# Linear attention into two MLPs on one core: the second batch's norms as rows through DRAM

## The chip, the cores and the metric

The kernel runs on one core of a Trainium2 chip, as one program. The metric is the device time of that program in microseconds (us). Before the change it is 1420.68 us, the median of three runs that lie between 1420.35 and 1421.77.

## What is computed

```
kv  = einsum('bhsd,bhse->bhde', k, v)            # 8 batches, 8 heads, 576 positions, 64 wide
out = einsum('bhsd,bhde->bhse', q, kv)
rms = sqrt(mean(out * out, axis=-1) + 1e-6)
x   = (out / rms * g_norm)                       # as 4608 tokens x 512
h   = x @ w_in;  x = (h * cos(h)) @ w_out        # 512 -> 2048 -> 512
a = x @ w1;  b = x @ w2                          # 512 -> 1024
result = ((a * b) @ w3) @ w_out2                 # 1024 -> 1024 -> 512
```

Everything is float32 outside. A product that has to be exact to float32 is made of three matrix products, with each operand cut into a high part (a copy in the fp32r type) and a low part (the operand less its high part).

## The kernel before, in words

A *unit* is half a batch: 288 tokens, units 0 and 1 are batch 0, units 2 and 3 batch 1. A *pair* p (0 to 3) is two heads, which fill the 128 partitions. A *block* is 512 tokens of the first MLP: block 0 is all of unit 0 and 224 tokens of unit 1, block 1 is 64 tokens of unit 1, unit 2, and 160 tokens of unit 3.

A *step* is one block of 512 tokens against 128 columns of w_in: `emit_h` issues its twelve matmuls (four slices c of the 512 inputs, three products each) on PE, ACT then rounds h/2pi to r (L619), DVE forms u from h and r (L620), ACT takes the sine of u (L636), and DVE multiplies it with h (L642). The first eight steps (h_0 to h_7) belong to block 0, the ninth (h_8) is the first of block 1. It reads the tile x_1, which needs the normalised output of the second batch. x is made from o (the attention's output) by a multiplication with the reciprocal norms, a copy to the high part on ACT (L910) and a subtraction for the low part (L911).

Weights come as *chunks*: a chunk is loaded as 64-bit words (`Chunk.load`), turned to floats in five operations (`Chunk.convert`: one on ACT at L156, four on DVE at L157, L158, L161 and L166), and then put: the high part on ACT (L122), the low part (L124) on DVE for the first four chunks and on GpSimd for the rest. Chunk i0 is w_in0 for step 0, and so on.

Batch 0 is done first (`first_batch`, L489). For each pair: k·v products on PE (`emit_kv`), their copy to a block diagonal on ACT (`copy_kv`), the output for both units (`emit_whole`, tile "out"), squares on ACT (`emit_square`), the sums of squares on PE into a narrow tile (`emit_sums`, tile "ms_first": 96 tokens down, 48 columns), and o kept on ACT (`emit_keep`). Then `norms` runs eleven small operations on DVE, and `emit_rows` spreads the norms over 64 partitions each by 12 small PE products for each unit and pair (tile "spread"), from which DVE scales o.

Batch 1 is woven into the first eight steps (`first_steps`, L565): its outputs, squares and sums lie one pair to a step in steps 0 to 3; `norms` follows in step 4, and the spreading and the scaling of o by DVE in steps 4 to 6, before h_8.

All engines execute in the order in which the code is written (the schedule is manual). SP's queue issues most DMAs in order, and each issue waits until the DMA eight places ahead of it has landed. So an instruction that waits holds up all that stand behind it on its engine.

Of the kernel before, what the change touches and what calls it, by code (L numbers as in the profile page):

```python
# [33 lines left out]
def kernel(  # L34
# [218 lines left out]
    rest_home = ap.tile([P, NPAIR // 2, 2, 2, P], F32, name="kvrest")  # L253

    def load_rest(b):
        t = kv_rest.setdefault(b, rest_home)
        for h in range(2):
            queue(NHALF * b).dma_start(
                out=t[0:TAIL, :, h], in_=kv_tail[b, TAIL * h:TAIL * (h + 1)]
            )  # L260
# [131 lines left out]
    def load_first():  # L392
# [15 lines left out]

        qs(0, 0, nc.scalar)
        qs(0, 1, nc.scalar)  # L410
# [4 lines left out]
        kv(0, 0, nc.sync)  # L415
        load_rest(0)
        kv(0, 1, nc.sync)
        prefetch(1)
        kv(0, 2, nc.sync)
        prefetch(2)  # L420
        qs(0, 2, nc.sync)
        prefetch(3)
        kv(0, 3, nc.sync)
        prefetch(4)
        qs(0, 3, nc.sync)
        for p in range(NPAIR):
            if p == 2:
                load_rest(1)
            kv(1, p, nc.sync)
        for p in range(NPAIR):  # L430
            qs(1, p, nc.sync)
            if p == 1:
                prefetch(8)
# [16 lines left out]
    def column(u, k, p):  # L450
        return ((u % NHALF * NT3 + k) * NPAIR + p) * 2
# [23 lines left out]
    def emit_rows(u, p, ps, y, spread, scaled=True):  # L475
        for k in range(NT3):
            at = column(u, k, p)
            for h in range(2):
                mm = nc.tensor.matmul(
# [4 lines left out]
        if scaled:  # L484
            o = o_sb[u][:, p, :]
            nc.vector.tensor_tensor(o, o, ps[:, 0:HALF], ALU.mult)
        return mm.ins

    def first_batch(spread, x, y, t):  # L489

        sums = ps_h.tile([P, 512], F32, tag="h", name="ms_first")
        units = range(NHALF)
        count = [1, 1, 1, 1]

        def pieces(n):
            made = [c.convert() for c in chunks[state["conv"]:state["conv"] + n]]
            state["conv"] += n
            for st in made:
                next(st)
            return made  # L500

        def rest_of(made):
            for _ in range(4):
                for st in made:
                    next(st)

        emit_kv(0, 0)
        copy_kv(0)
        made = None
        for p in range(NPAIR):  # L510
# [6 lines left out]
            if p == 0:  # L517
                made = pieces(count[0])
            if p < 3:
                rest_of(made)  # L520
            if p > 0:
                put(1)
# [9 lines left out]
            if p == 2:  # L532
                rest_of(pieces(count[3]))
            if p < 2:
                made = pieces(count[p + 1])
        for p in range(NPAIR):
            emit_kv(1, p)
            if p < 2:
                copy_kv(p)
        norms(sums, x, y, t)  # L540
        put(1)
        for p in (2, 3):
            copy_kv(p)
        for p in range(NPAIR + 1):
            if p < NPAIR:
                for u in units:
                    ps = ps_acc.tile(
                        [P, 512], F32, tag=f"acc{(2 * p + u) % 4}", name=f"spread_{u}_{p}"
                    )
                    emit_rows(u, p, ps, y, spread)  # L550
            if p == 0:
                for v in range(NHALF, 2 * NHALF):
                    out_bank(v, 0)
            if p > 0:
                split_x(0, p - 1)
# [9 lines left out]
    def first_steps(spread, x, y, t):  # L565

        units = range(NHALF, 2 * NHALF)
        spread_ps = {}
# [18 lines left out]
        def rows(p):  # L587
            for v in units:
                spread_ps[v, p] = two_banks(v, p, f"spread_{v}_{p}")
                emit_rows(v, p, spread_ps[v, p], y, spread, False)  # L590
# [1355 lines left out]
```

## Time and profile before

| | |
|---|---|
| median of 3 runs | 1420.68 us |
| the profiled execution's own time | 1422.03 us |
| its span | 1419.8 us |
| PE busy | 1401.1 us (99%) |
| DVE, ACT, POOL busy | 1004.3, 716.7, 568.6 us |
| chain of waits, by engine | PE 83%, DMA 5%, DVE 5%, POOL 2% |

The span is what lies between the first and the last instruction; the execution's own time holds 2.2 us more. PE is TensorE, DVE VectorE, ACT ScalarE, POOL GpSimd, SP the queue that issues DMAs; a q behind a name means that engine's issuing side. By the profile's windows, PE is busy 25.2 of the first 34.3 us, 34.2 of the next 34.4, and 1271.1 of the 1279.8 us from 140 us on. The chain of waits is the list of what each thing waited for last, followed back from the end. Where it names PE without a break, PE had work all the time, and every microsecond of PE work taken out or put in there moves the end.

### The profile page before, as it was taken

To read this page: it belongs to the slowest core of one execution; us is meant where nothing else is said; L and a number is where in the kernel's file an instruction comes from. 1 tells how busy PE (TensorE), PEld (TensorE's weight loads), DVE (VectorE), ACT (ScalarE), POOL (GpSimd) and SP (SyncE) were. 2 spreads that over 40 slices of the span, in tenths; PEclk is the share of its full clock that TensorE was granted. 3 is DMA by queue.
4 is the path that set the end of the run, shared out by engine and by line. 5 is a ranking of instruction groups with operands and counts; after the bars stand their busy time and mean duration, and the time that the engine had idled before them with its cause. 6 is when DMAs were issued, how large, how long until landed. Compare 5 with 4: busy or idle time off the path is not lost.

```text
span 1419.8 us, 23399 instructions
## 1 busy us (share of the span) xinstructions
PE 1401.1 (99%) x8376; PEld 1233.3 (87%) x8376; DVE 1004.3 (71%) x1555; ACT 716.7 (50%) x1338; POOL 568.6 (40%) x444
## 2 busy tenths in 40 slices
PE   7999999999999999999999999999999999999998
PEld 6877777777787888988888888999999999999998
DVE  5786575675778856888988957687775757855553
ACT  5665565545656655455555535443442334555553
POOL 1173763685385522132222428885760433100000
PEclk9999999999999999999999999999999999999999
DMA  9365987987798998999999982554445344775662
GB/s 338 130 232 171 338 258 220 300 281 247 240 320 305 324 345 294 319 348 326 371 334 358 363 298 103 159 158 139 140 134 149 97 144 144 248 273 216 252 219 101
DMA packets 210548, 345.55 MB, mean 243 GB/s; under 512 B 19104, under 2 KB 120576, under 8 KB 210048
## 3 DMA queue, kind: packets, MB, share of 16 engines
q1 hardware_dynamic: 209728, 343.48, 71.2%
q8 instruction: 65, 1.06, 0.3%
q10 hardware_dynamic: 704, 0.59, 0.1%
q14 instruction: 51, 0.42, 0.1%
HBM read 205.89 MB, written 138.11 MB: 242 GB/s over the span
## 4 chain that ended last, share of the span: by engine, by line
PE 83%; DMA 5%; DVE 5%; POOL 2%; issue 2%; ACT 1%; SPq 1%; ACTq 0%; DVEq 0%; POOLq 0%
PE X L1090 13%; PE X L1420 13%; PE h L916 8%; PE oX L1522 7%; PE h L917 7%; PE h L918 7%; PE V L1420 7%; PE V L1090 6%; PE oV L1522 4%; PE Y L1420 3%; PE Y L1090 3%; PE oY L1522 2%; PE event L297 1%; DMA g<-ta 1%; DVE g_hl L124 1%
## 5 line engine op out<-in xcount | busy, mean ns | idle before, releaser
L916 PE MATMUL h<-x,w_in 128*128 128x512 f32 x576 | 229.7, 399 | 1.3 <-DVE u L1740 0.9
L917 PE MATMUL h<-x,w_in 128*128 128x512 f32 x576 | 224.7, 390 | 0.7 <-DVE x L911 0.7
L918 PE MATMUL h<-x,w_in 128*128 128x512 f32 x576 | 224.6, 390 | 0.0
L1420 PE MATMUL X<-xc,w 128*128 128x384 f32 x1152 | 215.9, 334 | 0.7 <-ACT s L1428 0.6
L1420 PEld LDWEIGHTS X<-xc,w 128*128 128x128 f32 x1152 | 201.0, 188 | 1.4 <-ACT s L1428 1.4
L1090 PE MATMUL X<-g_hl,wl 128*128 128x512 f32 (+1 forms) x960 | 200.0, 368 | 0.1
L1090 PEld LDWEIGHTS X<-g_hl,wl 128*128 128x128 f32 x960 | 167.2, 189 | 30.8 <-DVE g_hl L124 0.6
L124 DVE TENSOR_TENSOR g_hl<-g_raw,g_hl 128x1024 fp32r<-128x1024 f32 x97 | 138.3, 1452 | 42.1 <-ACT g_hl L122 41.9
L124 POOL TENSOR_TENSOR g_hl<-g_raw,g_hl 128x1024 fp32r<-128x1024 f32 x29 | 73.7, 2541 | 231.7 <-ACT g_hl L122 202.8
L1766 DVE SCALAR_TENSOR_TENSOR u<-h,r 128x512 f32<-128x512 f32 x136 | 93.4, 687 | 92.4 <-ACT r L1765 70.7
L122 ACT ACTIVATE g_hl<-g_raw 128x1024 fp32r<-128x1024 f32 x126 | 130.5, 1057 | 55.6 <-DMA g_raw<-g 50.3
L1428 ACT ACTIVATE s<-X 128x384 f32<-128x384 f32 x144 | 70.7, 491 | 172.6 <-PE X L1420 172.6
L1765 ACT ACTIVATE r<-h 128x512 int32<-128x512 f32 x136 | 81.5, 599 | 124.3 <-PE h L918 123.9
L916 PEld LDWEIGHTS h<-x,w_in 128*128 128x128 f32 x576 | 108.0, 188 | 37.2 <-issue 5.8
L124 POOL TENSOR_TENSOR xc<-x2r,xc 128x768 fp32r<-128x768 f32 x49 | 97.2, 2011 | 102.6 <-ACT xc L122 102.4
L918 PEld LDWEIGHTS h<-x,w_in 128*128 128x128 f32 x576 | 108.1, 188 | 23.1
L917 PEld LDWEIGHTS h<-x,w_in 128*128 128x128 f32 x576 | 108.2, 188 | 22.9 <-DVE x L911 1.4
L1522 PE MATMUL oX<-wq,ab_hl 128*128 128x256 f32 x864 | 109.9, 283 | 0.5 <-ACT os L1532 0.5
L1420 PE MATMUL V<-xc,w 128*128 128x384 f32 x576 | 108.2, 335 | 1.1 <-DVE a L1472 1.0
L1522 PEld LDWEIGHTS oX<-wq,ab_hl 128*128 128x128 f32 x864 | 106.5, 192 | 0.7 <-ACT os L1532 0.7
L1420 PEld LDWEIGHTS V<-xc,w 128*128 128x128 f32 x576 | 100.3, 188 | 2.4 <-DVE a L1472 2.4
L1090 PE MATMUL V<-g_hl,wl 128*128 128x512 f32 (+1 forms) x480 | 100.4, 368 | 0.0
(194 smaller groups left out, 2417.8 us busy)
## 6 DMA issues: line engine op xcount, KB each, us to landing
g_raw<-g SPq DMA_DIRECT2D x126, 512.0 KB
ab_raw<-ab SPq DMA_DIRECT2D x34, 768.0 KB
ab<-q SPq DMA_DIRECT2D x96, 192.0 KB
kvraw<-in_kv_main_dram SPq DMA_DIRECT2D x32, 512.0 KB
g<-ta SPq DMA_DIRECT2D x32, 512.0 KB
g<-tb SPq DMA_DIRECT2D x32, 512.0 KB
g<-u SPq DMA_DIRECT2D x28, 512.0 KB
ab<-s SPq DMA_DIRECT2D x72, 192.0 KB
```

The lines of the kernel that those rows point to most:

```text
L122: hi = nc.scalar.activation(dst[:, 0], src, AF.Copy)
L124: lo = lo_engine.tensor_tensor(dst[:, 1], src, f32(dst[:, 0]), ALU.subtract)
L297: nc.tensor.matmul(ps[D * j:D * (j + 1), d], keys[:, d], values[:, d], start=i == 0 and h == 0, stop=i == NC, skip_group_check=True,)
L916: nc.tensor.matmul(ps, w[0], x[0], start=first, stop=False)
L917: nc.tensor.matmul(ps, w[0], x[1], start=False, stop=False)
L918: return nc.tensor.matmul(ps, w[1], x[0], start=False, stop=last).ins
L1090: nc.tensor.matmul(ps, w[:, a, i2, ws], g[:, b, q], start=first and half == 0 and q == 0 and n == 0, stop=last and final and q == KH - 1 a ...
L1420: nc.tensor.matmul(ps, w[:, self.i, a, k], x[:, b, k], start=first and k == 0 and n == 0, stop=last and k == 1 and n == 2, skip_group_chec ...
L1428: nc.scalar.activation(s, ps, AF.Copy)
L1522: nc.tensor.matmul(ps, t[:, a, k], w[:, b], start=first and k == 0 and n == 0, stop=last and k == 3 and n == 2, skip_group_check=True,)
L1765: nc.scalar.activation(r, h_ps[n], AF.Identity, bias=0.25, scale=INV_2PI)
L1766: nc.vector.scalar_tensor_tensor(u, h_ps[n], INV_2PI, r, ALU.mult, ALU.subtract)
```

## The change: what it does

In the diff's own order: the short rest of k and v (64 of 576 positions) lies on all 128 partitions for the first two batches and comes in one transfer a batch, where it came in two of 64 partitions; for later batches its two halves go to two halves of the partitions. The first loads are issued in another order. The norms of the first batch follow its last sums at once. The last two k·v products of batch 1 stand between the spreading of batch 0, not ahead of it. Two pairs' low parts of x go to GpSimd. Chunks i2 and i3 are converted later. Seven small products of ones run on PE ahead of all. The outputs of batch 1 for pairs 0 and 1 are made ahead of h_0. Its norms come in step 2; three PE products turn them to 16 rows of 288 (tile "turned"), ACT copies them, one DMA writes them to DRAM, and six DMAs read them back, each row spread over 64 partitions (tiles "bc"). GpSimd then multiplies o with bc (L389 and L641 of the changed kernel), in place of 96 PE products and 8 DVE operations. In h_0 to h_8 the four products with the low part of the weight (of x, in h_0 and h_8) come last.

```
         kv(0, 0, nc.sync)
         qs(0, 0, nc.scalar)
+        nc.sync.dma_start(out=kv_rest[0], in_=kv_tail[0])
...
-        rest = kv_rest[b][:, p // 2, p % 2]
+        if b < 2:
+            rest = kv_rest[b][TAIL * (p % 2):TAIL * (p % 2 + 1), p // 2]
...
+        norms(sums, x, y, t)
+        emit_kv(1, 0)
+        copy_kv(0)
+        emit_kv(1, 1)
+        copy_kv(1)
+        made = begin()
         for p in range(NPAIR):
-            emit_kv(1, p)
...
+                emit_rows(u, p, ps, y, spread)
+            if p in (1, 2):
+                emit_kv(1, p + 1)
+            split_x(0, p, lows=nc.gpsimd if p < 2 else nc.vector)
+            if p in (1, 2):
+                copy_kv(p + 1)
+            rest_of(made, 1)
         put(1)
...
+        for p in range(2):
+            for v in range(NHALF, 2 * NHALF):
+                out_bank(v, p)
+        for p in range(2):
+            for v in range(NHALF, 2 * NHALF):
+                emit_square(v, p)
+            for v in range(NHALF, 2 * NHALF):
+                emit_keep(v, p)
             if p == 0:
+                made = begin()
+        rest_of(made)
+        put(1)
...
+        def turn():
+            ps = ps_acc.tile([P, 512], F32, tag="acc2", name="turned")
+            wide = NHALF * NPAIR * 2
+            for k in range(NT3):
+                nc.tensor.matmul(
+                    ps[0:wide, T3 * k:T3 * k + T3], y[:, wide * k:wide * k + wide], spread,
+                    start=k == 0, stop=True, skip_group_check=True,
+                )
+            return ps[0:wide, 0:HALF]
+
+        def share(ps):
+            m = ap.tile([P, HALF], F32, tag="tmp", bufs=5, name="turned_sb")[0:ps.shape[0]]
+            nc.scalar.activation(m, ps, AF.Copy)
+            d = dram.tile([ps.shape[0], HALF], F32, name="rsd_second")
+            nc.sync.dma_start(out=d, in_=m)
...
+            for h in range(2):
+                nc.sync.dma_start(
+                    out=bc[a][D * h:D * h + D], in_=rows[0, h].partition_broadcast(D)
+                )
...
+        def scaled(p, s):
+            o = o_sb[b][:, p, s]
+            nc.gpsimd.tensor_tensor(o, o, bc[b, p // 2][:, p % 2, s], ALU.mult)
...
-        begins = (1, 1, 1, 0, 0, 0, 1, 0)
+        begins = (1, 0, 1, 1, 1, 0, 0, 0)
...
+            if n == 3:
+                turned = turn()
+            if n < HM - 1:
+                emit_h(n + 1, "acc3" if n % 3 == 1 else None)
+            else:
+                for c in (slice(0, 2), slice(2, KD)):
+                    split_x(1, c, (b,))
+                emit_h(HM)
...
+            if n == 5:
+                for p in range(NPAIR):
+                    emit_x(a, slice(p, p + 1), slice(0, HALF))
+            if n == 6:
+                for p in range(NPAIR):
+                    scaled(p, slice(0, first))
+                for c in (slice(0, 2), slice(2, KD)):
+                    split_x(1, c, (a,))
...
+        if n <= HM:
+            late = 1 if n in (0, HM) else 2
+            todo = [(c, k) for c in range(KD) for k in range(3) if k != late]
+            todo += [(c, late) for c in range(KD)]
```

Of what stands on an engine, three places matter below. The first is PE between the sums of batch 0 and h_0. Names end in unit, pair and a buffer number (kv, k and q: batch and pair). Before:

```order
L466 MATMUL ms_first_166<-sel_83,sq_1_3_306 96x2 x3
L278 MATMUL kv_1_0_319<-kvraw_1_0_140 64x64 x8
L278 MATMUL kv_1_0_319<-kvrest_1_98 64x64 x2
...
L278 MATMUL kv_1_3_356<-kvraw_1_3_148 64x64 x8
L278 MATMUL kv_1_3_356<-kvrest_1_98 64x64 x2
L479 MATMUL spread_0_0_385<-rs_first_100 64x96 x6
L479 MATMUL spread_1_0_393<-rs_first_100 64x96 x6
L445 MATMUL out_2_0_401<-q_1_0_150,rs_first_100 128x288
L445 MATMUL out_3_0_403<-q_1_0_150,rs_first_100 128x288
...
L479 MATMUL spread_1_3_454<-rs_first_100 64x96 x6
```

And of the change:

```order
L486 MATMUL spread_1_1_380<-rs_first_98 64x96 x6
L280 MATMUL kv_1_2_388<-kvraw_1_2_141 64x64 x8
L280 MATMUL kv_1_2_388<-kvrest_1_97 64x64 x2
L486 MATMUL spread_0_2_406<-rs_first_98 64x96 x6
L486 MATMUL spread_1_2_414<-rs_first_98 64x96 x6
L280 MATMUL kv_1_3_422<-kvraw_1_3_147 64x64 x8
L280 MATMUL kv_1_3_422<-kvrest_1_97 64x64 x2
L486 MATMUL spread_0_3_440<-rs_first_98 64x96 x6
L486 MATMUL spread_1_3_448<-rs_first_98 64x96 x6
L452 MATMUL out_2_0_464<-q_1_0_143,rs_first_98 128x288
L452 MATMUL out_3_0_466<-q_1_0_143,rs_first_98 128x288
L452 MATMUL out_2_1_468<-q_1_1_145,rs_first_98 128x288
```

The spreading of two pairs moved ahead of k·v for pairs 2 and 3, and a second pair's output stands ahead of h_0. The second place is ACT from the last high part of x_0 to r of step 0. Before:

```order
L910 ACTIVATE x_0_421<-o_1_187 128x224
L156 ACTIVATE i4_f_480<-i4_w_154 128x512
L457 ACTIVATE sq_2_0_509<-out_2_0_401 128x288
L457 ACTIVATE sq_3_0_512<-out_3_0_403 128x288
L619 ACTIVATE r_0_514<-h_0_482 128x512
```

And of the change, where w_in2 and w_in3 are the parts of chunks i2 and i3:

```order
L952 ACTIVATE x_0_366<-o_1_194 128x224
L122 ACTIVATE w_in2_461<-i2_f_348 128x512
L464 ACTIVATE sq_2_0_473<-out_2_0_464 128x288
L464 ACTIVATE sq_3_0_476<-out_3_0_466 128x288
L467 ACTIVATE o_2_472<-out_2_0_464,gneg_84 128x288
L467 ACTIVATE o_3_475<-out_3_0_466,gneg_84 128x288
L156 ACTIVATE i3_f_480<-i3_w_149 128x512
...
L122 ACTIVATE w_in3_492<-i3_f_480 128x512
L156 ACTIVATE i4_f_505<-i4_w_155 128x512
L667 ACTIVATE r_0_543<-h_0_507 128x512
```

Three operations stood between the last high part and r_0, now twelve do. The third place is GpSimd between the low parts of x_0 and block 1's u; before, w_in8 was the last there ahead of ta (the differences of u), and no x was made. Of the change:

```order
L953 TENSOR_TENSOR x_1_684<-o_1_194,x_1_684 128x4x64
L124 TENSOR_TENSOR w_in6_695<-i6_f_648,w_in6_695 128x512
L124 TENSOR_TENSOR w_in7_724<-i7_f_690,w_in7_724 128x512
L124 TENSOR_TENSOR w_in8_751<-i8_f_719,w_in8_751 128x512
L389 TENSOR_TENSOR o_2_472<-o_2_472,bc_2_675 128x288 x4
L641 TENSOR_TENSOR o_3_475<-o_3_475,bc_3_0_678 128x160 x2
L641 TENSOR_TENSOR o_3_475<-o_3_475,bc_3_1_681 128x160 x2
```

All the multiplications of unit 2 and those of unit 3 that block 1 needs stand behind the low part of w_in8.

## Rows read from the trace of the kernel before

**Rows 1.** Chain of waits: start us, us, what.
```profile
66.57 2.13 PE spread L479 x48
68.70 0.43 PE h L916
71.65 0.23 PE h L916
41.55 1.08 PE out L445 x4
```

**Rows 2.** Timeline of PE: start us, us, engine, line, operation [idle before <-releaser].
```profile
7.80 0.48 PE L278 MATMUL kv<-kvrest 128*64 128x64 f32 x4 [2.12 <-DMA kvrest<-in_kv_tail_dram]
8.94 2.26 PE L445 MATMUL out<-q,rs_first 128*128 128x288 f32 x4 [0.65 <-issue]
21.26 1.20 PE L466 MATMUL ms_first<-sel,sq 128*96 128x2 f32 x12
24.57 0.48 PE L278 MATMUL kv<-kvrest 128*64 128x64 f32 x4 [1.06 <-DMA kvrest<-in_kv_tail_dram]
31.20 3.19 PE L479 MATMUL spread<-rs_first 96*64 96x96 f32 x72
```

**Rows 3.** Windows: us, busy of PE, PEld, DVE, ACT, POOL; PEclk, DMA share, GB/s.
```profile
6.00:8.00 2.00, 0.20 (x4) 0.23 (x4) 0.00 (x0) 0.00 (x0) 0.00 (x0) 1.00 1.03 193
8.00:10.00 2.00, 1.35 (x6) 0.93 (x5) 0.00 (x0) 0.44 (x2) 0.00 (x0) 1.00 1.04 383
20.00:22.00 2.00, 1.91 (x13) 1.35 (x13) 1.93 (x5) 1.94 (x5) 0.00 (x0) 1.00 1.08 246
26.00:28.00 2.00, 1.80 (x30) 1.56 (x29) 1.02 (x3) 1.31 (x5) 0.00 (x0) 0.50 1.07 388
28.00:30.00 2.00, 2.00 (x43) 1.91 (x40) 0.36 (x1) 0.63 (x3) 0.00 (x0) 0.72 1.04 412
```

**Rows 4.** Timeline of ACT and DVE around the end of x_0.
```profile
34.90 0.81 DVE L486 TENSOR_TENSOR o<-o,spread 128x288 f32<-128x288 f32 x2
35.37 0.76 ACT L910 ACTIVATE x<-o 128x288 fp32r<-128x288 f32 x2 [0.64 <-DVE o L486]
36.03 0.66 ACT L156 ACTIVATE i_f<-i_w 128x512 f32<-128x512 f32 x1
37.90 0.60 ACT L619 ACTIVATE r<-h 128x512 int32<-128x512 f32 x1 [0.46 <-PE h L918]
```

**Rows 5.** Timeline of ACT, DVE and POOL over step 2 and the start of step 3.
```profile
47.22 0.58 ACT L619 ACTIVATE r<-h 128x512 int32<-128x512 f32 x1
47.84 0.69 DVE L620 SCALAR_TENSOR_TENSOR u_first<-h,r 128x512 f32<-128x512 f32 x1 [1.18 <-ACT r L619]
49.10 0.69 ACT L457 ACTIVATE sq<-out 128x288 f32<-128x288 f32 x2
50.26 0.88 ACT L460 ACTIVATE o<-out,gneg 128x288 f32<-128x288 f32 x2
51.40 0.63 ACT L122 ACTIVATE w_in<-i_f 128x512 fp32r<-128x512 f32 x1 [0.27 <-DVE i_f L166]
51.93 0.58 ACT L619 ACTIVATE r<-h 128x512 int32<-128x512 f32 x1
52.10 1.30 POOL L124 TENSOR_TENSOR w_in<-i_f,w_in 128x512 fp32r<-128x512 f32 x1 [3.41 <-ACT w_in L122]
```

**Rows 6.** Timeline of DVE: the second batch's norms, first and last of 11, and the next step.
```profile
57.86 0.19 DVE L472 TENSOR_SCALAR rs_first<-ms_second 96x48 f32<-96x48 f32 x1
60.22 0.20 DVE L353 SCALAR_TENSOR_TENSOR rs_first<-rs_first 96x48 f32<-96x48 f32 x1
60.95 0.68 DVE L620 SCALAR_TENSOR_TENSOR u_first<-h,r 128x512 f32<-128x512 f32 x1
```

**Rows 7.** Timeline of SP and POOL: a later unit's rows read back, and x from them.
```profile
282.96 1.30 SPq L379 DMA_DIRECT2D bc<-rsd  x2
289.61 3.12 POOL L384 TENSOR_TENSOR o<-o,bc 128x288 f32<-128x288 f32 x4 [5.42 <-DMA bc<-rsd]
```

More of the change, by code (lines that the diff above doesn't have):

```diff
@@ L257, in load_rest, with tail @@
         for h in range(2):
-            queue(NHALF * b).dma_start(
-                out=t[0:TAIL, :, h], in_=kv_tail[b, TAIL * h:TAIL * (h + 1)]
-            )
+            tail(b, h)
+    def tail(b, h):
+        rows = slice(TAIL * h, TAIL * (h + 1))
+        nc.sync.dma_start(out=kv_rest[b][rows, h], in_=kv_tail[b, rows])
     def load_kv(b, p, tag=None):
@@ L419, in load_first @@
         kv(0, 2, nc.sync)
+        qs(0, 2, nc.sync)
         prefetch(2)
-        qs(0, 2, nc.sync)
+        kv(0, 3, nc.sync)
+        qs(0, 3, nc.sync)
+        nc.sync.dma_start(out=kv_rest[1], in_=kv_tail[1])
+        kv(1, 0, nc.sync)
+        kv(1, 1, nc.sync)
         prefetch(3)
-        kv(0, 3, nc.sync)
+        kv(1, 2, nc.sync)
+        qs(1, 0, nc.sync)
+        qs(1, 1, nc.sync)
+        kv(1, 3, nc.sync)
         prefetch(4)
[L425 to L433, printed above, removed]
+        qs(1, 2, nc.sync)
+        qs(1, 3, nc.sync)
+        prefetch(8)
     whole = []
@@ L473, in norms, with emit_rows @@
         return newton(x, y, t)
-    def emit_rows(u, p, ps, y, spread, scaled=True):
+    def emit_rows(u, p, ps, y, spread):
         for k in range(NT3):
@@ L483, in emit_rows, with begin, rest_of @@
                 )
[L484 to L487, printed above, removed]
+        o = o_sb[u][:, p, :]
+        nc.vector.tensor_tensor(o, o, ps[:, 0:HALF], ALU.mult)
     def first_batch(spread, x, y, t):
         sums = ps_h.tile([P, 512], F32, tag="h", name="ms_first")
+        ones = row("ones")
+        nc.vector.memset(ones[:, 0:P], 1.0)
+        idle = ps_h.tile([P, 512], F32, tag="h", name="idle")
         units = range(NHALF)
[L493 to L499, printed above, removed]
-            return made
[L502 to L505, printed above, removed]
+        def begin():
+            c = chunks[state["conv"]]
+            state["conv"] += 1
+            made = c.convert()
+            next(made)
+            return made
+        def rest_of(made, count=4):
+            for _ in range(count):
+                next(made)
+        for _ in range(7):
+            nc.tensor.matmul(
+                idle[:, 0:D], ones[:, 0:P], ones[:, 0:D], start=True, stop=True,
+                skip_group_check=True,
+            )
         emit_kv(0, 0)
         copy_kv(0)
-        made = None
         for p in range(NPAIR):
@@ L1839, in run @@
                     f()
-        nc.gpsimd.memset(rest_home[TAIL:], 0.0)
+        for h in range(2):
+            nc.gpsimd.memset(rest_home[TAIL * (1 - h):TAIL * (2 - h), h], 0.0)
         with tc.manual_schedule(
```

143 lines of the change are left out of this document (60 added, 83 removed).

## The prediction

> **What bounds the kernel now.** I read the table of busy times first: PE is busy 1401.1 of 1419.8 us, so the end moves with whatever PE loses or gains. The chain of waits comes next. From the spreading of batch 0's norms on it names PE alone: the spread products end at 34.4 us (31.20 and 3.19) [rows 2], h_8 begins at 68.70 straight behind the last spread products of batch 1, and ends at 71.65 [rows 1]. Between 34.4 and 71.65 PE never runs dry, so all that this change does is judged by one number: when h_8 ends. Behind h_8 the steps are the same as before.
>
> Ahead of 34.4 us PE waits: 2.12 us for the rest of k and v of batch 0, 1.06 for that of batch 1 [rows 2]. The windows say why. While such a transfer is under way the DMA engines are full (share over 1) but move 193 and 246 GB/s, against 383 and 388 at other times [rows 3].
>
> The timeline of the steps shows a second loop, which nearly fills PE's time without being the bound: r of step 2 begins at 47.22, r of step 3 at 51.93, so 4.71 us a step [rows 5]. In it ACT rounds, DVE forms u, converts a chunk in four operations, and ACT copies the chunk's high part, behind which the next r stands in ACT's queue. A step without the attention's products takes PE only 2.95 us (68.70 to 71.65) [rows 1]. The first place to look is therefore whether, once PE has less to do, this loop becomes the bound.
>
> **The change, part by part: up to the last spread product.** One transfer in place of two for the rest of k and v: at 383 in place of 193 GB/s the 2 us would carry 0.38 MB more, which is 1.0 us [rows 3]; I take 1.0 off the 2.12 us wait (between 0 and 2.12). Batch 1's rest now comes behind fewer chunk loads, and its 1.06 goes. Two chunks fewer are converted in this stretch, which I count at 0.5 (0 to 1). So the last sums of batch 0, which ended at 22.46 (21.26 and 1.20) [rows 2], end at about 21.0. The norms follow at once: 57.86 to 60.42, or 2.56 us [rows 6], so 23.5. Then PE has four spreads, 1.07 each (half of 2.13) [rows 1], and two k·v sums of 20 matmuls, 1.2 each (30 matmuls took 1.80 at clock 0.50) [rows 3]: 6.7 us. The last spread ends at 30.2, against 34.4: 4.2 us won. Its bounds are 28.2 (both waits gone, full clock) and 32.2 (no transfer is faster: 22.46 + 2.56 + 6.7, with 0.5 for waits).
>
> **From there to r of step 0.** Before, that took 3.5 us (34.4 to 37.90 [rows 4]). Now ACT has twelve operations there where it had three. Scaling and high part of the last pair: from 34.90 to 36.13, with a start of 0.1, 1.35 us [rows 4]. DVE then makes the low part (0.37, an estimate from the 0.41 of a scaling, 0.81 for two [rows 4]) and the last operation on chunk i2 (0.7): 2.4 us. ACT: high part of w_in2 0.53 (51.40 to 51.93), two squares 0.69, two kept outputs 0.88 [rows 5], the first operation of i3 about 0.6 (0.66 [rows 4]): 5.1. DVE's four operations on i3 take 2.35 (3.56 us from u to the high part, 47.84 to 51.40 [rows 5], less u itself and the product, some 0.6 each): 7.45. High part of w_in3 and the first operation of i4: 8.6 us. PE does not wait in this time, but r_0 comes at 30.2 + 8.6 = 38.8, later than the 37.90 of before, although PE began 4.2 us earlier.
>
> **From r of step 0 to the end of h_8.** Steps 0 and 1 convert a chunk: 2 x 4.71. Step 2 has the norms: 0.62 to u, 0.61 to the norms (as 60.95 less a product of the same length), and 57.86 to 60.95, 3.09, to the next u: 4.3 in all [rows 5, 6]. So u of step 3 begins at r_0 + 13.7. Steps 3 and 4 convert again, 2 x 4.71: u of step 5 at r_0 + 23.15. It converts i8; the high part begins 3.56 later, GpSimd's low part 0.7 behind that and takes 1.30 [rows 5]: r_0 + 28.7. Only now does GpSimd come to x, since w_in8 stands ahead of it in its queue: four multiplications of 288 columns in 3.12 us [rows 7], four of 160 in about 2.0 (by columns 1.7, at full price 3.1), then 0.5 for the last high part on ACT: r_0 + 34.3. Of h_8's twelve products four can run before, eight remain, 1.95 us by 2.95 for twelve. h_8 ends at r_0 + 36.2; before it was 71.65 - 37.90 = 33.75. With r_0 = 38.8 that is 75.0, so 3.4 us later than before.
>
> What is removed is thereby hidden. The 96 spread products of batch 1, 4.26 us (2 x 2.13), and one pair of outputs, 1.08, leave PE's stretch [rows 1]. But PE would be ready for h_8 at 30.2 + 2 x 1.08 for the outputs + 34.3 (34.4 to 68.70) - 4.26 - 1.08, about 61.4, and by the turning of the norms at r_0 + 13.2 = 52.0, with four steps of 2.8 to 2.95 behind it, at some 63.5. It then stands still until about 72. The 8 scalings are off DVE, but the loop is tied by waiting for each other and not by DVE's sum. The trip through DRAM is hidden: two such loads had landed 6.65 us after their issue (282.96 to 289.61) [rows 7]; from the turning at 52.0, with a copy and a store, unit 2's rows are there at about 61, unit 3's at most as long again later, 67.7, when GpSimd is at w_in8 until 67.5 and then busy with unit 2 for 3.1 us. Cover gone, each microsecond of delay counts in full.
>
> **The clock.** PE's waits ahead of 26 us stand beside a granted clock of 0.50, 1.2 in place of 2.4 GHz, in 26 to 28 us, with 0.72 in the next 2 us, once PE had been full [rows 3]. A wait of some 8 us ahead of h_8 is longer than any of those. If all of h_8 ran at the low level, its twelve products would cost 2.8 us more (12 x 0.23 by 2.95 for twelve); if none did, nothing. I take 1.1, nearer the lower half, as four of the twelve run inside the wait.
>
> The Trainium skill has a rule for this (TensorE: Matmul & The Clock Gate, "What's actually happening"): the low clock is the default, and it is activity that lifts it. By that rule h_8 begins at the low level, and the sum would be up to 1426.9 us; by a clock that stays up it would be 1424.1.
>
> **Sum.** 4.2 won up to the last spread, 5.1 lost up to r_0 (8.6 against 3.5), 2.45 lost up to the end of h_8, 1.1 by the clock: 4.5 us later. The profiled execution spans 1419.8 us and lasts 1422.03, 2.2 around the span and 1.35 above the median; I put the difference to both alike: a span near 1424.3 and a median of 1420.7 + 4.5 = 1425.2. For the chain of five steps I allow 1.4 less, if they run shorter without squares between, and 1 more. The forecast's own range is 1422.5 to 1428.5.
>
> **Rivals.** *PE stays the bound (faster).* If the steps run as fast as PE feeds them and x_1 is ready in time, h_8 begins at 61.4 and ends at 64.4: 7.2 earlier, 1413.5 us. It needs a loop of about 3 us a step. For it: DVE is rid of 8 scalings, and GpSimd is idle for most of this stretch. Against it: ACT began r of step 3 right behind the high part of a chunk, 0.53 after it [rows 5]; it did not wait for PE then, and that order is kept. 0.17.
>
> *The early start pays for the rest (no change).* Last spread at 28.2 (2.0), clock stays up (1.1), the five steps 1.4 shorter: 4.5 lost become 0, 1420.7 us. For it: transfers of batch 0 and 1 are the only waits of PE at the start. Against: it takes all three together, or most of two. 0.23.
>
> *The DRAM trip is late (much slower).* If the six loads came one pair behind the other at 6.65 us each, unit 3's last rows would land at 52.0 + 2.3 + 20 = 74.3, against 70.6 when GpSimd wants them: it decides from 16 us for the six on, and at 20 costs 3.7 more, 1428.9 us. Against: the loads are issued one behind the other without a wait between. 0.05.
>
> **How the numbers follow.** Forecast 0.55, rivals 0.17, 0.23 and 0.05. What can be told from no change is 0.2%, 2.8 us, so 1417.8 to 1423.5. Slower: 0.05 and most of the forecast, 0.49. Same: 0.06 of the forecast and 0.18 of the second rival. Faster: the first rival and 0.05 of the second. The range 1417.0 to 1428.8 leaves out the first rival's middle and the third's.
>
> **What would show it.** Right: in the changed kernel PE's longest wait in the first 100 us stands at h_8, for ACT or GpSimd, some 8 us; r's of steps 3 to 5 lie 4.7 us apart; x of unit 2 on GpSimd begins right behind w_in8, with no wait for bc; the last spread ends near 30 us; the granted clock falls around h_8. Wrong: h_8 straight behind h_7; r's some 3 us apart; or a GpSimd that waits for bc.

## The result and the profile after

The changed kernel takes 1434.18 us (median of 6 runs, 1431.76 to 1437.81), the kernel before 1422.17 (6 runs beside it, 1420.35 to 1427.96): ratio 1.0079, 95% interval 1.0053 to 1.0105. It is slower, as forecast, but by 12.0 us, not 4.5, and outside the range (1417.0 to 1428.8). Of the 9.0 us between the forecast's 1425.2 and 1434.18, 1.5 are the base: the forecast started from 1420.7, and the kernel before took 1422.17 beside the change. The profiled execution took 1437.02 us with a span of 1435.2; that of before 1422.03 and 1419.8.

The timeline of PE in the changed kernel, columns as in [rows 2]:
```profile
6.18 0.48 PE L280 MATMUL kv<-kvrest 64*64 64x64 f32 x4
7.32 2.26 PE L452 MATMUL out<-q,rs_first 128*128 128x288 f32 x4 [0.66 <-issue]
18.51 2.27 PE L452 MATMUL out<-q,rs_first 128*128 128x288 f32 x4
26.17 1.97 PE L473 MATMUL ms_first<-sel,sq 128*96 128x2 f32 x12
31.00 4.11 PE L486 MATMUL spread<-rs_first 96*64 96x96 f32 x48
39.68 2.19 PE L486 MATMUL spread<-rs_first 96*64 96x96 f32 x24
41.79 3.46 PE L452 MATMUL out<-q,rs_first 128*128 128x288 f32 x8
84.24 5.09 PE L978 MATMUL h<-x,w_in 128*128 128x512 f32 x12 [8.53 <-ACT x L952]
```
The rows count two for each small float32 product of the code (one filler of e9 below shows as x2), so the 12 and the 96 spread products named ahead of the prediction are 6 and 48 in the code; no time depends on it. The waits for kvrest are gone, and the first pair of outputs starts 1.6 us earlier than in [rows 2]. But it takes 2.26 us, and so does every later pair up to 24.11, where before only the first did. The sums end at 28.1 (before 22.46), and 24 spread products take 2.1 to 2.2. The last ends at 41.87; before it was 34.39, and 30.2 was forecast. At the other end of the stretch stands a wait of 8.53 us and an h_8 of 5.09.

The windows of the same execution (us, busy of PE, PEld, DVE, ACT, POOL; PEclk, DMA share, GB/s):
```profile
12.00:22.00 10.00, 10.00 (x67) 7.56 (x67) 4.98 (x9) 5.26 (x13) 0.00 (x0) 1.00 1.03 397
22.00:32.00 10.00, 10.00 (x84) 8.72 (x84) 3.02 (x13) 4.73 (x14) 0.00 (x0) 1.00 0.90 269
74.00:82.00 8.00, 1.71 (x8) 1.09 (x6) 5.05 (x8) 3.22 (x6) 4.59 (x7) 0.78 0.76 244
82.00:92.00 10.00, 7.76 (x25) 6.22 (x26) 5.78 (x9) 3.59 (x7) 4.83 (x8) 0.66 0.27 93
```
From 7.3 us to the end of the opening PE has no idle time, and it completes little: 67 instructions from 12 to 22 us. The column of the granted clock reads 1.00 there, while the durations in the timeline are about twice those of the fast stretches (2.27 against 1.22 for a pair of outputs). The durations decide: 48 spread products take 4.11 us here, and the same 4.11 in e1 below, where the column reads 0.50. So this is the low level, 1.2 GHz.

ACT and POOL of the changed kernel in the steps (first and last r's, the way into x_1):
```profile
50.06 0.58 ACT L667 ACTIVATE r<-h 128x512 int32<-128x512 f32 x1
72.55 0.58 ACT L667 ACTIVATE r<-h 128x512 int32<-128x512 f32 x1
77.25 0.58 ACT L667 ACTIVATE r<-h 128x512 int32<-128x512 f32 x1
77.43 1.27 POOL L124 TENSOR_TENSOR w_in<-i_f,w_in 128x512 fp32r<-128x512 f32 x1 [3.41 <-ACT w_in L122]
78.65 3.05 POOL L389 TENSOR_TENSOR o<-o,bc 128x288 f32<-128x288 f32 x4
81.65 3.00 POOL L641 TENSOR_TENSOR o<-o,bc 128x160 f32<-128x160 f32 x4
84.68 0.47 ACT L952 ACTIVATE x<-o 128x320 fp32r<-128x320 f32 x1 [0.50 <-POOL o L641]
```
The steps are 4.70 apart, as in [rows 5]; x of unit 2 starts right behind w_in8's low part without a wait for bc; the last high part begins 34.6 us behind r_0 and ends 35.1 behind it. h_8 begins at 84.24, so 0.9 us ahead of that end.

Four marks divide each profiled execution, in us: the end of the last spread product, r of step 0, the first product of h_9 (the end of h_8's turn on PE), the end of the span.

| kernel | last spread | r_0 (behind it) | h_9 (behind r_0) | span (behind h_9) |
|---|---|---|---|---|
| before | 34.39 | +3.51 | +33.58 | 1419.8 (+1348.3) |
| after | 41.87 | +8.19 | +39.11 | 1435.2 (+1346.0) |

So the span's 15.4 us are 7.5 in the opening, 4.7 up to r_0, 5.5 in the steps, less 2.3 behind h_9, where the changed kernel's rest is shorter.

### The profile page after: what moved, and what is told of

Its sections match the earlier page's. It is cut to its first block, busy times and chain, and to the rows that moved or that the text cites. A ratio compares the mean times of both kernels' runs of the same rounds, so it can differ in the third digit from the quotient of the medians.

```text
span 1435.2 us, 23243 instructions
## 1 busy us (share of the span) xinstructions
PE 1415.4 (99%) x8300; PEld 1245.6 (87%) x8300; DVE 1000.5 (70%) x1536; ACT 717.7 (50%) x1332; POOL 582.0 (41%) x460
## 3 DMA queue, kind: packets, MB, share of 16 engines
q8 instruction: 65, 1.06, 0.3%
## 4 chain that ended last, share of the span: by engine, by line
PE 88%; DVE 4%; DMA 3%; ACT 2%; issue 2%; POOL 2%; SPq 0%; DVEq 0%; ACTq 0%; POOLq 0%
PE X L1142 14%; PE X L1472 12%; PE h L958 8%; PE h L959 7%; PE h L960 7%; PE oX L1574 7%; PE V L1142 7%; PE V L1472 6%; PE oV L1574 4%; PE Y L1142 3%; PE Y L1472 3%; PE oY L1574 2%; PE event L302 1%; PE event L729 1%; DMA kvrest<-in_kv_tail_dram 1%
## 5 line engine op out<-in xcount | busy, mean ns | idle before, releaser
L958 PE MATMUL h<-x,w_in 128*128 128x512 f32 x540 | 214.5, 397 | 0.8 <-DVE u L1792 0.7
L960 PE MATMUL h<-x,w_in 128*128 128x512 f32 x540 | 210.5, 390 | 0.0
L959 PE MATMUL h<-x,w_in 128*128 128x512 f32 x540 | 210.4, 390 | 0.0
L1142 PEld LDWEIGHTS X<-g_hl,wl 128*128 128x128 f32 x960 | 167.3, 189 | 30.2 <-DVE wl L124 0.2
L124 POOL TENSOR_TENSOR g_hl<-g_raw,g_hl 128x1024 fp32r<-128x1024 f32 x29 | 78.0, 2690 | 227.6 <-ACT g_hl L122 166.3
L958 PEld LDWEIGHTS h<-x,w_in 128*128 128x128 f32 x540 | 101.3, 188 | 34.9 <-issue 6.2
L960 PEld LDWEIGHTS h<-x,w_in 128*128 128x128 f32 x540 | 101.4, 188 | 21.8
L959 PEld LDWEIGHTS h<-x,w_in 128*128 128x128 f32 x540 | 101.4, 188 | 20.0
```

The costliest lines, as they stand in the source:

```text
L124: lo = lo_engine.tensor_tensor(dst[:, 1], src, f32(dst[:, 0]), ALU.subtract)
L958: nc.tensor.matmul(ps, w[0], x[0], start=first, stop=False)
L959: nc.tensor.matmul(ps, w[0], x[1], start=False, stop=False)
L960: return nc.tensor.matmul(ps, w[1], x[0], start=False, stop=last).ins
L1142: nc.tensor.matmul(ps, w[:, a, i2, ws], g[:, b, q], start=first and half == 0 and q == 0 and n == 0, stop=last and final and q == KH - 1 a ...
```

## The experiments

Each is the changed kernel with the edit shown, unless it says otherwise. "Before" in a comparison is the kernel before, run beside it; its medians in the five comparisons were 1422.2, 1423.1, 1422.3, 1423.6 and 1422.3.

**Is the slow opening the rule? e12, e13 (the changed kernel) and e14 (the kernel before), as they are.**

> The changed kernel as it is, a second profile. Theory A (TensorE's clock in the opening differs from execution to execution, and the time with it): of the first six times two lay at 1437 to 1438 and four at 1431.8 to 1434.9; a profile of the second kind shows the opening's pairs of outputs speed up from 2.26 to 1.22 some way in, the last spread product 3 to 6 us ahead of 41.9, and the span shorter by nearly as much. Theory B (the opening is slow throughout in every execution): last spread product at 41.9 again, whatever the time.

> The changed kernel as it is, a third profile. Theory A: as for the second; the span less the start of h_9 stays at 1346 within 1 us, so that what the time does is what the opening does. Theory B: last spread product at 41.9 again.

> The kernel before as it is, a second profile. Theory A (its clock in the opening differs too, and that is why its times run from 1419.6 to 1429.8): the last spread product ends elsewhere than at 34.4, and the time differs from 1422.0 by about as much. Theory B (its opening is stable, its times differ by what comes later): last spread product within 0.5 us of 34.4 whatever the time.

Times 1433.79, 1432.22 and 1424.10 us; spans 1432.0, 1430.4, 1422.2. The timeline of PE in e13:
```profile
12.96 2.27 PE L452 MATMUL out<-q,rs_first 128*128 128x288 f32 x4
17.41 1.22 PE L452 MATMUL out<-q,rs_first 128*128 128x288 f32 x4
22.93 2.08 PE L473 MATMUL ms_first<-sel,sq 128*96 128x2 f32 x12 [1.24 <-ACT sq L464]
27.86 4.11 PE L486 MATMUL spread<-rs_first 96*64 96x96 f32 x48
34.98 1.21 PE L486 MATMUL spread<-rs_first 96*64 96x96 f32 x24
```
and in e14:
```profile
8.42 0.48 PE L278 MATMUL kv<-kvrest 128*64 128x64 f32 x4 [2.27 <-DMA kvrest<-in_kv_tail_dram]
20.35 2.27 PE L445 MATMUL out<-q,rs_first 128*128 128x288 f32 x4
25.06 1.22 PE L445 MATMUL out<-q,rs_first 128*128 128x288 f32 x4
33.78 3.19 PE L479 MATMUL spread<-rs_first 96*64 96x96 f32 x72
```

| kernel | last spread | r_0 | h_9 | span |
|---|---|---|---|---|
| e12 (after) | 38.81 | +8.18 | +38.73 | 1432.0 (+1346.3) |
| e13 (after) | 36.19 | +8.56 | +39.45 | 1430.4 (+1346.2) |
| e14 (before) | 36.97 | +3.52 | +33.58 | 1422.2 (+1348.1) |

Theory A holds for both kernels. The point at which the products become fast differs from execution to execution (changed kernel: about 42, 16 and 16 us; before: 12 and 24), and so does the end of the opening; the other three parts repeat within 0.8 us. In e12 and e13 the products slow down again at 23, behind a wait of 1.24 us for ACT's squares; in e13 they speed up at about 33, in e12 only with the outputs at 38.73. Averaged over the profiles shown, the opening ends at 39.0 in the changed kernel and 35.7 in the one before: 3.3 us later, not 4.2 earlier.

**e1: a denser start** (three products of 128x512 ones instead of seven of 128x64).
```
-        nc.vector.memset(ones[:, 0:P], 1.0)
+        nc.vector.memset(ones, 1.0)
-        for _ in range(7):
-                idle[:, 0:D], ones[:, 0:P], ones[:, 0:D], start=True, stop=True,
+        for _ in range(3):
+                idle, ones[:, 0:P], ones, start=True, stop=True,
```


> The change, with three products of 128 x 512 ones in place of the seven of 128 x 64 at the start of PE. Theory A (the opening ran at half clock from end to end, and this is the part of the loss that was not forecast): with denser work at the start the clock rises early, the pairs of outputs fall from 2.3 to 1.2 us, the last spread product ends near 31 us and not at 41.9, and the time falls by 8 to 11 us against the change, to 1423 to 1426. Rival B (the opening is slow by its new order of loads and products, whatever the clock): same as the change, 1434 within 2.

1431.45 us (1429.72 to 1433.47), ratio 1.0044 (1.0024 to 1.0065); span 1427.9. PE in e1:
```profile
8.17 1.21 PE L452 MATMUL out<-q,rs_first 128*128 128x288 f32 x4 [0.66 <-issue]
20.03 2.08 PE L473 MATMUL ms_first<-sel,sq 128*96 128x2 f32 x12 [0.89 <-ACT sq L464]
24.97 4.11 PE L486 MATMUL spread<-rs_first 96*64 96x96 f32 x48
32.06 1.21 PE L486 MATMUL spread<-rs_first 96*64 96x96 f32 x24
75.97 5.45 PE L978 MATMUL h<-x,w_in 128*128 128x512 f32 x12 [8.52 <-ACT x L952]
```
and its window of the 48 spread products:
```profile
24.00:28.00 4.00, 4.00 (x54) 3.77 (x54) 1.87 (x7) 1.92 (x6) 0.74 (x1) 0.50 1.05 386
```
The outputs are fast from the first pair on, and the last spread ends at 33.27, 8.6 us ahead of the profile of after. But from 20 to 30, behind the last outputs and a wait of 0.89 us for ACT's squares, PE is slow again, at a granted clock of 0.50. The three products of ones also have a price: they hold the first k·v product back from 4.91 to 6.57. The rest of the table is unchanged (r_0 +8.56, h_9 +39.43, end +1346.6). So in these profiles the level of the clock decides when the opening ends. The median's gain of 2.7 is under the 8 to 11 expected, and the two ratios' intervals overlap.

**e2: without the seven products.**
```
-        for _ in range(7):
-            nc.tensor.matmul(idle[:, 0:D], ones[:, 0:P], ones[:, 0:D], ...)
```


> The change without the seven products of ones on PE. Theory A (the clock stays low because the opening's own work is thin; the seven products are too small to matter): same as the change, 1434 within 3. Rival C (the seven products themselves put the opening on the wrong foot, and without them it runs as before the change): the clock rises near 12 us, the last spread product ends near 31 us, 1423 to 1426.

1432.35 us (1431.72 to 1436.26), ratio 1.0067 (1.0044 to 1.0090). Its profile has the first fast pair at 11.95, slow work from 20.5 on, the last spread at 36.14, and a span of 1429.9. That lies beside the fastest of the three profiles of the changed kernel (36.19 and 1430.4), and the time is Theory A's: the seven products are not what makes its opening slow. Rival C's rise near 12 us came, but not its end near 31 us or its time.

**e9: the clock held through the opening and at h_8** (e8, below, and six more products of 128x512 ones).
```
+            if p + 1 == NPAIR:
+                fill(1)
             for u in units:
                 emit_sums(u, p, sums, fresh=True)
...
         emit_kv(1, 0)
         copy_kv(0)
+        fill(1)
         emit_kv(1, 1)
         copy_kv(1)
+        fill(1)
...
                 emit_rows(u, p, ps, y, spread)
+            if p < 3:
+                fill(1)
```


> The run with the dense start and the held clock at h_8, and six more products of 128x512 ones in the stretch of the opening in which TensorE went slow in the runs with the dense start (20 to 33): one ahead of the last pair's sums, one behind each of batch 1's first two state products, one behind each of the first three pairs' spread products; some are covered by waits (0.9 to 1.25 us for ACT's squares, 0.9 for DVE's norms), the others cost 0.85 each. Theory A (the failed step is TensorE's clock in the opening: with 1.07 to 1.2 per 24 spread products and 1.02 per pair's state the forecast's own sum holds): spreads take 2.2 per 48, the last spread product ends near 31 where it ended at 35.5, h_9 starts 4 us earlier than in the run with held clock, near 77, and the time is 1425 to 1427, the forecast being 1425.2. Theory B (another wait takes the place: loads, DVE's or ACT's work on the pairs): the spreads are fast, but PE waits for DVE or ACT between them, the last ends at 34 or later, and the time is 1429 or more.

1429.22 us (1426.12 to 1433.89), ratio 1.0038 (1.0023 to 1.0053); span 1426.1. PE in e9:
```profile
19.05 1.02 PE L515 MATMUL idle<-ones 128*128 128x512 f32 x2
24.08 1.12 PE L515 MATMUL idle<-ones 128*128 128x512 f32 x2
25.14 1.21 PE L486 MATMUL spread<-rs_first 96*64 96x96 f32 x24
33.48 1.21 PE L486 MATMUL spread<-rs_first 96*64 96x96 f32 x24
77.16 3.08 PE L992 MATMUL h<-x,w_in 128*128 128x512 f32 x12 [0.48 <-ACT x L961]
```
and its window of the stretch that was slow in e1:
```profile
22.00:32.00 10.00, 10.00 (x125) 6.12 (x126) 4.96 (x17) 3.99 (x12) 3.09 (x4) 1.00 1.05 396
```
Every spread and every sum is at the high level now, and the last spread ends at 34.69. The DMA engines move as much in this window (396 GB/s) as in the slow one of the changed kernel from 12 us on (397), so the loads' traffic is not what halves PE's pace. The six fillers take 6.64 us in the timeline; without them, and with the waits of 0.9 and 0.9 that e1 and e7 show there, it would end near 29.9 (worked out, not run). That is close to the 30.2 of the forecast: its sum nearly holds for a clock that this order of work doesn't get by itself (the first k·v product comes 2.0 us later than in the changed kernel, at 6.91, and the k·v products are faster than the sum had them). What holds the clock up costs about as much as it brings. Theory A's time (1425 to 1427) was reached by two of the twelve runs; the median and the end of the opening are Theory B's (1429 or more, 34 or later), but with fillers where it put waits. By the ratios e9 can't be told from e8 or e1.

**e4: the steps alone** (loads and opening as before; squares and kept outputs of batch 1's first two pairs behind it; the new steps).
```
             if p > 0:
                 split_x(0, p - 1)
+        for v in range(NHALF, 2 * NHALF):
+            out_bank(v, 1)
+        for p in range(2):
+            for v in range(NHALF, 2 * NHALF):
+                emit_square(v, p)
+            for v in range(NHALF, 2 * NHALF):
+                emit_keep(v, p)
```


> The loads and the work on batch 0 as in the kernel before, with the outputs, squares and kept outputs of batch 1 for pairs 0 and 1 added at its end, and the steps of the change. Theory A: the opening ends at 34.4 us as before, r of step 0 comes at about 40, h_8 ends 39 later, at 79 against 71.65: some 5 to 7 us above the kernel before, 1426 to 1428, so that about 5 to 6 of the 11 us of loss are the opening's. Rival (all the loss is in the steps): 1432 to 1434.

1428.45 us (1424.93 to 1430.91), ratio 1.0034 (1.0019 to 1.0049); span 1424.8: last spread 34.69, r_0 +5.03, h_9 +39.14, end +1345.9. The marks are Theory A's (34.4, about 40, 39 later); the median lies 0.5 above its range.

**e7: the opening alone** (new loads, new opening with the dense start; steps as before).
```
-        for p in range(2):
-            for v in range(NHALF, 2 * NHALF):
-                out_bank(v, p)
-        for p in range(2):
...
-            if p == 0:
-                made = begin()
+        for v in range(NHALF, 2 * NHALF):
+            out_bank(v, 0)
+        made = begin()
         rest_of(made)
```


> The new loads and the new opening of batch 0 with the dense start, but the eight steps as before (norms of batch 1 spread by TensorE into each pair's bank, multiplied on DVE; no trip through DRAM, no norm work of batch 1 in the opening beyond the first pair's products). Theory A (the steps cost about 5 us by the chain of ACT, DVE and GpSimd ahead of h_8, the opening costs by its clock alone): last spread product at 32 to 34 when the clock is up, h_8 within 1 us of before's 68.7, and the time within 2 us of before's, 1421 to 1424. Theory B (the opening's order and loads cost by themselves, 4 us or more): h_8 at 72 or later and 1427 or more.

1429.50 us (1424.93 to 1434.42), ratio 1.0061 (1.0043 to 1.0078). The profiled execution is its fastest; span 1423.0: last spread 34.78, r_0 +7.43, h_9 +34.88, end +1345.9. ACT in e7, ahead of r_0:
```profile
36.76 0.63 ACT L122 ACTIVATE w_in<-i_f 128x512 fp32r<-128x512 f32 x1 [1.06 <-DVE i_f L166]
40.40 0.63 ACT L122 ACTIVATE w_in<-i_f 128x512 fp32r<-128x512 f32 x1 [2.44 <-DVE i_f L166]
42.21 0.60 ACT L631 ACTIVATE r<-h 128x512 int32<-128x512 f32 x1
```
Theory A's time fell, and Theory B's came (1427 or more). Even with old steps, r_0 stands 7.4 us behind the last spread, since the fourth chunk's conversion was moved in between: the opening costs by its order too, not by its clock alone. e7 has the dense start, so e1 is its partner: 0.61% with the old steps, 0.44% with the new ones, and the intervals overlap. Behind this opening the medians do not show the price of the new steps that e4 shows alone (0.34%), and it is not shown that the parts add up.

**e8: the clock held at h_8** (dense start, and 36 products into h_8's bank ahead of its own).
```
+            for _ in range(36 if n == HM else 0):
+                nc.tensor.matmul(
+                    ps, w_in[0][:, 0, 0], x_hl[0][:, 0, 0], start=True, stop=True,
+                    skip_group_check=True,
+                )
```


> The changed kernel with the dense start, and 36 products of 128x512 with the weights of w_in 0 in TensorE's row ahead of h_8's own, into h_8's bank, which the first of its own starts afresh: TensorE is busy in some 8 of the 8.5 us in which it waits for x. Theory A (the low clock at h_8 is a price of the wait): h_8 takes 3 us rather than 5.45, h_9 starts 2 to 2.5 us earlier after r of step 0, and the time is 1429 to 1430 against 1431.45 of the dense start alone. Theory B (what h_8 loses comes back later, or TensorE's clock doesn't follow these products): h_8 stays at 4.5 us or more, or the time stays at 1431 to 1432.

1429.56 us (1427.71 to 1431.69), ratio 1.0053 (1.0040 to 1.0066); span 1427.2. PE in e8:
```profile
69.28 8.32 PE L976 MATMUL h<-x,w_in 128*128 128x512 f32 x36
78.09 3.08 PE L983 MATMUL h<-x,w_in 128*128 128x512 f32 x12 [0.49 <-ACT x L952]
```
h_8 takes 3.08 instead of 5.45, and h_9 comes 37.21 behind r_0 instead of 39.43: the clock at h_8 is worth 2.2 to 2.4 us by the profile. By the ratios the two kernels can't be told apart, so what it is worth in time isn't shown.

**e3: x ahead of w_in8** (GpSimd's multiplications of units 2 and 3 ahead of w_in8's low part), **and e6: the same with the dense start.**
```
-            put(len(group))
             if n == 5:
                 for p in range(NPAIR):
                     emit_x(a, slice(p, p + 1), slice(0, HALF))
+                for p in range(NPAIR):
+                    scaled(p, slice(0, first))
+            put(len(group))
```


> The change, with the multiplications of x for units 2 and 3 ahead of the low part of w_in8 in GpSimd's queue. Theory D (x waits behind the conversion of chunk i8): the rows are back from DRAM by then, h_8 begins some 3.5 us earlier, 1434 - 3.5 = 1430.5. Rival E (the trip through DRAM ends only when GpSimd comes to x): GpSimd waits for bc at that place, gain below 1 us.

> The changed kernel with the dense start (three products of 128x512) and with GpSimd's multiplications of units 2 and 3 ahead of w_in8's low part, which each were tried alone. Theory A (costs add along the path to h_8): h_8 starts 2.4 us earlier after the last spread product than in the run with the dense start alone, so near 73.5 if the opening ends at 33.2, and the time is 1429 (1431.45 less 2.4). Theory B (what is won ahead of h_8 is given back later, as the profile of the run with x first alone suggested): h_8 is earlier by the same 2.4 and the time stays at 1431 to 1432.

e3: 1432.16 us (1428.20 to 1437.43), ratio 1.0063 (1.0041 to 1.0084); e6: 1430.15 (1424.57 to 1430.56), 1.0044 (1.0028 to 1.0060). In the profiles h_9 comes 36.17 and 37.16 behind r_0 (after 39.11, e1 39.43), 2.3 to 2.9 earlier, and GpSimd does not wait for bc although it asks for it some 4.7 us sooner behind r_0: Theory D's mechanism, not rival E's. The rest is 1349.3 and 1347.5, 3.3 and 0.9 longer than in after and e1. That the gain is given back there is not shown: among profiles with the steps of the kernel before, the rest also differs by 1.7 (e11 1347.8, e5 1349.5). By the ratios e3 can't be told from after, nor e6 from e1, and e6's time agrees with neither theory clearly. DVE and POOL in e3:
```profile
74.03 4.34 POOL L389 TENSOR_TENSOR o<-o,bc 128x288 f32<-128x288 f32 x4
74.39 0.92 DVE L158 TENSOR_SCALAR i_f<-i_f 128x512 int32<-128x512 int32 x1
76.55 1.17 DVE L166 SCALAR_TENSOR_TENSOR i_f<-i_w,i_f 128x512 int32<-128x512 int32 x1
```
The same operations took 3.05, 0.43 and 0.69 in the changed kernel, where they did not meet. e6 repeats it (4.34, 0.92 and 1.16). The third integer operation of DVE in this stretch (L161) kept its 0.70.

**e15: the fourth conversion moved from behind the last spread into step 3** (dense start).
```
-            if p == 0:
-                made = begin()
-        rest_of(made)
-        put(1)
...
-        begins = (1, 0, 1, 1, 1, 0, 0, 0)
+        begins = (1, 0, 2, 1, 1, 0, 0, 0)
```


> The changed kernel with the dense start, and the fourth conversion of w_in words moved from behind the last spread product into step 3 (the steps begin one conversion more). Theory A (ACT's row behind the last spread holds r of step 0 by its conversions: of 8.2 us from the last spread to r_0 TensorE's outputs and h_0 take 6.2 and two conversions 2.0): r_0 starts 6.2 to 6.6 us after the last spread product, but step 3 has two conversions and takes up to 2.4 us more, so that h_9 moves by less than 1 us and the time stays at 1431 to 1432. Theory B (the extra conversion fits into ACT's and DVE's waits of step 3): h_9 2 us earlier, 1429.

1433.34 us (1428.30 to 1434.98), ratio 1.0067 (1.0048 to 1.0086). r_0 comes 5.89 behind the last spread (e1 8.56), so the conversion does cost 2.7 us there. But PE now waits inside the steps:
```profile
62.09 5.73 PE L974 MATMUL h<-x,w_in 128*128 128x512 f32 x24 [2.87 <-ACT w_in L122]
```
and h_9 comes 43.3 behind r_0 (41.56 to 84.88; e1 39.43): 1.2 us are lost in sum. Theory A, slightly worse than it said.

**e5, e10, e11: parts alone on the kernel before** (the dense start; the tails of k and v in one transfer, ahead; both). The core of e10:
```
+        kv(0, 0, nc.sync)
         qs(0, 0, nc.scalar)
+        nc.sync.dma_start(out=kv_rest[0], in_=kv_tail[0])
         qs(0, 1, nc.scalar)
...
-        kv(0, 0, nc.sync)
-        load_rest(0)
```


> The kernel before, with three products of 128x512 ones ahead of its first product; nothing else differs. Theory A (TensorE's low clock in the opening is a cost of its own, whatever the order of the opening): before's record shows out at 2.26 us up to 8.94 and 1.22 from 13.30, then slow again from 22 to 28; with the dense start the first pairs take 1.2 and the last spread product ends up to 2 us earlier than 34.4. Time 1420 to 1423, at most 2 us under before of the same batch, since its loads bound the first 8 us. Theory B (the new opening is slow by its order and its loads, and clock decides nothing): the last spread ends within 0.5 us of 34.4 and the time equals before's.

> The kernel before with one part of the change alone: the tails of k and v of batches 0 and 1 in one transfer of 128 partitions each, ahead of the others, and the first pair's k, v ahead of q on the queues. The waits of TensorE for kvrest, 2.12 at 7.80 and 1.06 at 24.57, should go. Theory A (the opening of before is bound by TensorE behind its first state, at either clock): the last spread product ends 1.5 to 3 us ahead of 34.4 and the time is 1419 to 1421 against 1422.3. Theory B (what is won at 7.8 is lost at the next load, q of pair 3, as with the dense start alone): the wait for q at 20 grows by as much, and the time is before's within 0.2%.

> The same part alone on the kernel before, with the dense start. Theory A (the first state's wait was what kept the dense start from paying): the last spread product ends 3 to 4 us ahead of 34.4 and the time is 1418 to 1420. Theory B (loads bind next): q of pair 3 and the tails of batch 1 are waited for, and the time stays within 0.2% of before's.

e5: 1422.55 us, ratio 1.0003 (0.9991 to 1.0015); e10: 1423.80, 1.0007 (0.9992 to 1.0022); e11: 1424.94, 1.0011 (0.9995 to 1.0026). None gains, so the times are Theory B's in all three. In e10 the waits for kvrest are gone, but the profiled execution stays slow until 22, and its last spread ends at 39.29:
```profile
6.40 0.48 PE L280 MATMUL kv<-kvrest 64*64 64x64 f32 x4
18.73 2.27 PE L449 MATMUL out<-q,rs_first 128*128 128x288 f32 x4
36.10 3.19 PE L483 MATMUL spread<-rs_first 96*64 96x96 f32 x72
```
In e5 the first pairs are fast, but the q of pair 3 is waited for 1.06 us at 20.30 (0.33 before), and the last spread ends at 35.85; in e11 PE is slow again from 17.5 on, and it ends at 37.72. In all three, r_0 (+3.5) and h_9 (+33.6) repeat the kernel before. No run beats it.

e10 also shows a price of the one transfer that the forecast put at nothing: the last four of a pair's 20 k·v products are of 64 partitions instead of 128. From the first product of such a group to the sums behind it, both at the low level, in e10 and then in e14:
```profile
15.33 1.12 PE L280 MATMUL kv<-kvraw 128*64 128x64 f32 x16
16.79 2.08 PE L470 MATMUL ms_first<-sel,sq 128*96 128x2 f32 x12
17.14 1.12 PE L278 MATMUL kv<-kvraw 128*64 128x64 f32 x16
18.41 2.08 PE L466 MATMUL ms_first<-sel,sq 128*96 128x2 f32 x12
```
That is 1.46 us against 1.27; at the high level it is 0.88 in e11 against 0.73 in e5. For the eight groups of the opening this makes 1.2 to 1.5 us (an estimate, eight times the difference).

## Why the prediction was wrong in size

**The step that failed: the last spread product at 30.2.** Measured 41.87, and 38.81 and 36.19 in two more executions; outside the bounds 28.2 to 32.2. The two transfers did land early: in the profile PE waits for neither kvrest. What failed is the price of the work behind them. The forecast took 1.07 for 24 spread products, which is their price at the high level, and let the sums end 1.5 earlier as if the pairs kept the pace of before; in the profile the spread products cost 2.1 to 2.2 and each pair of outputs 2.26. The 20 k·v products had been priced at the low level (1.2) and took 1.5 (1.27 in e14, with the old layout of the rest): the new layout made them longer, which the forecast put at nothing. e9 shows that at the high level the sum nearly holds (29.9, worked out), e1 that this order of work, even with a fast first half, ends at 33.3. The rows to see it by were there: [rows 3] had the granted clock at 0.50 and 0.72 at 26 to 30 us of the kernel before, where the first spread products run, and [rows 2] a pair of 2.26 at 8.94. One execution of before was taken for its rule; e14 shows another that is slow until 24. In sum the opening ends 3.3 us later (mean of the profiles) instead of 4.2 earlier: 7.5 us. That this equals the difference between the 4.5 forecast and the 12.0 measured to a tenth is luck: it rests on three profiles and two that differ among themselves by several us, and the other terms cancel only because the rest behind h_8 came out shorter.

**From there to r_0: right.** 8.2 to 8.6 against 8.6. e7 and e15 name the part: the conversion stands ahead of r_0 on ACT, at 2.7 us.

**From r_0 to the end of h_8: the mechanism right, the last term short by 2.0.** Steps 4.70 apart (4.71), w_in8's low part on GpSimd done at r_0 + 28.6 (28.7), PE's longest wait at h_8 (8.53 for some 8). Some four of h_8's products do run ahead of the end of the last high part where the level is high, as forecast (e8); at the low level two do. Two terms were too small. GpSimd's four multiplications of 160 columns were put at 2.0 us, as e3 has them (1.96), but took 3.00, two of them beside DVE's low parts of x: the last high part ends at r_0 + 35.1, 0.8 late. And h_8 ends at r_0 + 39.3 (39.6 in e1), against 37.4 in e8, which holds the clock up: 1.9 to 2.2 for the clock, where 1.1 was put. The 36.2 forecast without the clock was 1.2 short of e8. By the rule of the Trainium skill that the prediction weighed (TensorE: Matmul & The Clock Gate, "What's actually happening") h_8 begins at the low level; 5.09 against 2.95 in [rows 1] agrees with it, and the rule would have served better than the middle value.

**Behind h_8: "the same as before" is not quite so.** The rest is 1346.0 to 1346.3 in three profiles of the changed kernel and 1348.3 and 1348.1 in two of before: 2.1 us less. e7, with the old steps, has 1345.9 too, and e4, with the old opening, as well, but e3 has 1349.3, so it is not shown to be the change's. By the windows behind h_9, PE is idle for 7.6 us in the changed kernel, 9.4 in before and 9.5 in e3: most of the difference lies in PE's waits. What sets them stays open. That it roughly pays for the 2.0 missed at h_8 is luck.

**The rivals.** PE as the bound fell: it waits 8.53 us. The early start that pays for the rest fell on its first condition. The DRAM trip is hidden, as forecast: GpSimd does not wait for bc, not even in e3, which asks for it sooner.

## What to carry to other kernels

Before an opening is shortened on paper, price its products at both levels of the clock, and look at two or three profiles of the same kernel: an engine that is busy without a gap may still be at half pace, and the pace can differ from execution to execution. Work that is taken off the bound engine shows up where the next loop ends: here in a chain of ACT, DVE and GpSimd whose 4.7 us a step did not change, so that PE's shorter row became a wait, with a slow product behind it. A transfer that lands sooner need not bring time: taken alone (e10) it gave nothing, for the products behind it were slow in that profile and its layout made some of them longer.

## What the runs showed of the hardware

- The record of the granted clock can read 1.00 while the durations are those of the low level: 12 to 22 us of the changed kernel, 2.27 for what takes 1.22 elsewhere. PE was busy without idle time from 7.3 to 42 us there and became fast only during the outputs at 41.79.
- Identical programs get the high level at different times (16 and 42 us; before 12 and 24), and the time follows: spans 1430.4, 1432.0 and 1435.2 for openings that end at 36.2, 38.8 and 41.9.
- Filling a wait with products kept the level up: 36 of them ahead of h_8 made it 3.08 us instead of 5.45. In e1, e12 and e13 the level fell behind waits of 0.89 and 1.24 us for ACT's squares; in e9, with a filler in that wait, it did not.
- GpSimd's multiplications and two of DVE's integer operations were slower where they met: 3.05 to 4.34, 0.43 to 0.92 and 0.69 to 1.17 us (e3, e6). Four multiplications of 160 columns took 1.96 in e3 and 3.00 beside DVE's low parts of x.
- The last four of 20 k·v products on 64 partitions instead of 128 made the group longer: 0.88 instead of 0.73 us at the high level, 1.46 instead of 1.27 at the low one.
